# Loading one weight matrix in two transfers, split by partitions: 16 rows and 112 rows

## The chip, the cores and the metric

The kernel runs on one core of one Trainium2 chip. The metric is the device time of one execution in microseconds (us), as the median of several runs. The record sorts runs into a fast and a slower state. The engines are called PE (matmuls), DVE (VectorE), ACT (ScalarE), POOL (GpSimd) and SP (SyncE, which here only issues transfers). The page of the profile counts 16 DMA engines, and they carry out a large transfer side by side: in `before` the first 16 rows of the first one begin between 1.84 and 2.78 us, each of them before any row has ended (3.27 us). In this text a "row" of a transfer is what goes to one partition of the on-chip memory (SBUF).

## The reference, cut to what matters

One decode step of a transformer block for eight sequences: a modulation (adaLN) from a condition `c`, attention over a key and value cache of 8192 positions, and a small MLP.

```python
mod = (_silu(c) @ w_mod).reshape(8, 6, 1, -1)          # w_mod: 512 x 3072, bf16, 3 MB
sa, ca, ga, sb, cb, gb = (mod[:, i] for i in range(6))
h = layernorm(x) * (1 + ca) + sa
x = x + ga * attention(h, k_cache, v_cache, wq, wo)    # caches: 2 x 8 x 8 x 8192 x 128, bf16, 268 MB
h = layernorm(x) * (1 + cb) + sb
return x + gb * mlp(h, w1, b1, w2, b2)
```

Nearly all of the bytes are the two caches. The modulation weights `w_mod` are about 1% of the total, and the change touches nothing but how they are loaded.

## The kernel before

The kernel streams everything through four slots of one SBUF buffer, `RING`, of 32 KB per partition and slot. SP issues the transfers in this order: `w_mod` into slot 2, `wq` into slot 3, the first two key units into slots 0 and 1, two small biases, `wo`, and then unit after unit as slots come free.

```python
d_wm = dma("sync", s_wm, lambda e: e.dma_start(
    RING[:, 2, 0:KT * NMOD], w_mod.rearrange("(p k) n -> p (k n)", k=KT)))
d_wq = dma("sync", s_wq, lambda e: e.dma_start(
    RING[:, 3, :], A_wq.rearrange("(p k) n -> p (k n)", k=KT)))
# ...
wmod_v = RING[:, 2, 0:KT * NMOD].rearrange("p (k n) -> p k n", k=KT)
# ... the first matmuls that need w_mod; they wait for all of it:
t = row_groups(bank(0), csT, wmod_v, (0, 1), [k_csT, d_wm])
k_mr0 = op("vector", lambda e: e.tensor_copy(mod_r[0:64, 0, :], bank(0)[0:64, :]), [t])
t = row_groups(bank(1), csT, wmod_v, (2, 3, 4, 5), [])
released[2] = t                      # slot 2 is free for the third key unit
# ...
t0 = row_groups(bank(2), haT, wq_v, (0, 1, 2, 3), [k_haT, d_wq])
# ...
load(0); load(1)                     # 4 MB key units
# ... two biases, wo
load(2); load(3)                     # these wait for released[2], released[3]
```

In `w_mod` each partition gets one contiguous row of 24,576 bytes (KT x NMOD = 4 x 3072 numbers of 2 bytes); in `wq` and in each cache unit it gets one row of 32,768 bytes. The helper `dma` adds 16 to the wanted value of its semaphore with every transfer, so two transfers on `s_wm` are waited for together: a wait for 32 passes only when both have landed.

## Time and profile before

| | before |
|---|---|
| time, median of 3 runs | 669.88 us (669.33 to 670.03) |
| span of the profiled run | 667.6 us |
| PE busy | 513.8 us (77%) |
| DMA moved | 283.85 MB, 425 GB/s over the span |
| `w_mod` landed, from issue | 10.3 us |

The page's slices come first: the span in 40 equal parts, the busy share of the 16 DMA engines in tenths, and the rate.

```profile
DMA  9999999999999999999999999999999999999996
GB/s 376 431 412 437 426 427 435 432 430 430 434 434 430 430 432 436 428 432 432 436 428 430 434 434 430 430 434 434 428 432 434 434 426 434 432 434 428 434 415 264
```

All slices but the last are at 90% or more, and the packets of SP's queue alone fill 99.1% of the 16 engines' span (packets, MB, share):

```profile
q1 hardware_dynamic: 12116, 283.65, 99.1%
```

That points to the transfers as what sets the time. The page's chain of waits, followed back from the last instruction, is less plain, for by shares PE has more of it than the transfers:

```profile
PE 52%; DMA 37%; ACT 7%; DVE 2%; SPq 1%; issue 1%
```

Shares can't decide it, because SP's queue is full while PE works. The longest links of the chain are these; the columns are start in us, length in us, and what was waited for.

```profile
1.26 13.33 DMA ring<-in_A_wq_dram
14.59 46.84 DMA ring<-in_A_k_cache_dram
...
95.68 24.03 DMA ring<-in_A_k_cache_dram
...
561.59 24.42 DMA ring<-in_A_k_cache_dram
...
649.42 14.74 DMA ring<-in_B_w_dram
```

At the beginning and in every batch (one sequence) the longest link is a wait for key data, and the chain ends in a wait for the last weights of the MLP, `B_w`. SP issues far ahead: a key load lands 34 us after its issue (the page's list of transfers). So the engines always have work queued.

The timeline shows the start: start in us, length in us, engine, line, operation, what it writes and reads, and in brackets how long the engine had been idle and for whom.

```profile
0.81 0.39 SPq L286 DMA_DIRECT2D ring<-in_w_mod_dram  x1
...
1.26 0.42 SPq L288 DMA_DIRECT2D ring<-in_A_wq_dram  x1
...
11.33 3.21 PE L398 MATMUL PS<-ring,KTb 128*32 128x512 bf16 x24
...
21.27 3.36 PE L398 MATMUL PS<-ring,KTb 128*32 128x512 bf16 x32 [3.76 <-DMA ring<-in_A_wq_dram]
...
30.71 5.53 PE L479 MATMUL PS<-IDENT,ring 128*128 128x128 bf16 x64 [5.12 <-DMA ring<-in_A_k_cache_dram]
```

The modulation matmuls (the first line of PE, L398) start at 11.33 us, those with `wq` at 21.27, and the first key tiles at 30.71. The list of transfers has these two entries (KB, and us from issue to landing):

```profile
ring<-in_A_wq_dram SPq DMA_DIRECT2D x1, 4096.0 KB, 19.9
...
ring<-in_w_mod_dram SPq DMA_DIRECT2D x1, 3072.0 KB, 10.3
```

Last, the same stretch in windows of 4 us; the last two columns are the DMA engines' busy share and the rate.

```profile
core 0: us, PE busy (x) PEld busy (x) DVE busy (x) ACT busy (x) POOL busy (x), PEclk, DMA share, GB/s
2.00:6.00 4.00, 0.29 (x4) 0.21 (x4) 0.85 (x2) 2.94 (x3) 3.38 (x9) 1.00 0.77 313
6.00:10.00 4.00, 0.27 (x4) 0.18 (x4) 1.18 (x5) 0.20 (x1) 3.71 (x3) 1.00 1.03 442
10.00:14.00 4.00, 3.24 (x26) 1.60 (x28) 1.35 (x3) 0.00 (x0) 2.58 (x11) 1.00 1.04 451
14.00:18.00 4.00, 3.51 (x22) 2.93 (x18) 1.08 (x5) 0.60 (x1) 2.19 (x12) 0.93 0.99 426
18.00:22.00 4.00, 0.73 (x8) 0.34 (x12) 0.00 (x0) 0.00 (x0) 2.26 (x12) 0.50 0.94 403
```

After a slow start the rate is that of the whole run. Below the views lie the records of the single packets; one packet is one row. They are given here as averages over 16 consecutive packets, that is about one row of each of the 16 engines:

```
before, w_mod (24,576 bytes each), us: 1.61 0.93 0.97 0.91 0.91 0.91 0.91 0.91
before, wq    (32,768 bytes each), us: 1.21 1.21 1.21 1.21 1.21 1.21 1.21 1.21
```

24,576 bytes in 912 ns are 26.9 GB/s for one engine and 431 GB/s for 16. No packet of the whole trace is faster than 27.04 GB/s, so each engine runs at the highest rate that is seen here, and nothing suggests that one hinders another. Only the first rows, at the start of the stream, take longer: 1.42 to 2.17 us, but for two of 0.99.

### The profile page before, as it was taken

The numbers are of one execution on the slowest core, as the hardware profiler recorded it, in microseconds if no ns is written. First come the engines' busy times: TensorE is split into PE (matmuls) and PEld (weight loads), VectorE is DVE, ScalarE is ACT, GpSimd is POOL, SyncE is SP. The second block draws the span as 40 slices with busy tenths as digits, with TensorE's granted clock in tenths as the row PEclk, the third lists the DMA queues.
The fourth block names the chain that finished last, engine by engine and source line by source line (L and its number), as shares of the span: only waits on it lengthen the run. The fifth ranks groups of instructions, "written<-read, shape, count | busy, mean of one in ns | idle before, by whom it ended". The sixth has DMA issues, their size and how long they took to land.

```text
span 667.6 us, 15485 instructions
## 1 busy us (share of the span) xinstructions
PE 513.8 (77%) x7064; PEld 344.8 (52%) x7064; DVE 302.6 (45%) x571; ACT 258.7 (39%) x289; POOL 18.4 (3%) x76
## 2 busy tenths in 40 slices
PE   3493984898739985699848987499756998389885
PEld 2283731675328742577317853287425773177534
DVE  2262731566216651367314662166513673156722
ACT  2151640466105660266404662066502654046610
POOL 7300000000000000000000000000000000000000
PEclk9696997899969998699977999699987999779996
DMA  9999999999999999999999999999999999999996
GB/s 376 431 412 437 426 427 435 432 430 430 434 434 430 430 432 436 428 432 432 436 428 430 434 434 430 430 434 434 428 432 434 434 426 434 432 434 428 434 415 264
DMA packets 12176, 283.85 MB, mean 425 GB/s; under 512 B 1250, under 2 KB 1283, under 8 KB 3588
## 3 DMA queue, kind: packets, MB, share of 16 engines
q1 hardware_dynamic: 12116, 283.65, 99.1%
q8 instruction: 9, 0.15, 0.1%
q10 hardware_dynamic: 48, 0.02, 0.0%
q14 instruction: 3, 0.02, 0.0%
HBM read 283.66 MB, written 0.01 MB: 425 GB/s over the span
## 4 chain that ended last, share of the span: by engine, by line
PE 52%; DMA 37%; ACT 7%; DVE 2%; SPq 1%; issue 1%
PE PS L479 36%; DMA ring<-in_A_k_cache_dram 32%; PE PS L496 9%; ACT P_sb L562 5%; PE PS L616 2%; DMA ring<-in_B_w_dram 2%; DMA ring<-in_A_wq_dram 2%; PE PS L469 1%; SPq L659 1%; ACT KTb L484 1%; DVE O_sb L626 1%; PE PS L463 1%; PE PS L574 1%; DVE Pm L588 0%; PE PS L594 0%
## 5 line engine op out<-in xcount | busy, mean ns | idle before, releaser
L484 ACT ACTIVATE KTb<-PS 128x1024 bf16<-128x1024 bf16 x192 | 196.5, 1024 | 332.2 <-PE PS L479 332.2
L479 PE MATMUL PS<-IDENT,ring 128*128 128x128 bf16 x4096 | 267.4, 227 | 51.2 <-DMA ring<-in_A_k_cache_dram 51.2
L479 PEld LDWEIGHTS PS<-IDENT,ring 128*128 128x128 bf16 x4096 | 246.8, 102 | 99.6 <-DMA ring<-in_A_k_cache_dram 52.4
L486 DVE COPY KTb<-PS 128x1024 bf16<-128x1024 bf16 x320 | 210.1, 687 | 143.9 <-PE PS L479 141.8
L616 PE MATMUL PS<-ring,Pm 128*32 128x512 bf16 x992 | 70.4, 434 | 46.8 <-DMA ring<-in_A_v_cache_dram 45.9
L496 PE MATMUL PS<-KTb,Qb 128*32 128x512 bf16 x1024 | 78.8, 385 | 4.5 <-ACT KTb L484 4.5
L626 DVE CAST O_sb<-PS 128x512 bf16<-128x512 f32 x31 | 21.4, 692 | 126.7 <-PE PS L616 126.7
L616 PEld LDWEIGHTS PS<-ring,Pm 128*32 128x32 bf16 x992 | 26.8, 106 | 85.5 <-DMA ring<-in_A_v_cache_dram 54.4
L562 ACT ACTIVATE P_sb<-PS,negm 128x1024 bf16<-128x1024 f32 x32 | 35.2, 1112 | 20.2 <-DVE negm L557 20.2
L469 PE MATMUL PS<-ONES 128*128 128x512 f32 x80 | 42.1, 630 | 0.0
L574 PE MATMUL PS<-IDENT,P_sb 128*128 128x128 bf16 x256 | 19.9, 220 | 15.4 <-ACT P_sb L562 15.4
L588 DVE COPY Pm<-PS 64x512 bf16<-64x512 bf16 x48 | 20.2, 421 | 25.0 <-PE PS L574 24.5
L574 PEld LDWEIGHTS PS<-IDENT,P_sb 128*128 128x128 bf16 x256 | 14.4, 98 | 25.1 <-ACT P_sb L562 25.1
L463 PE MATMUL PS<-IDENT 128*128 128x512 bf16 x88 | 26.9, 380 | 0.0
L496 PEld LDWEIGHTS PS<-KTb,Qb 128*32 128x32 bf16 x1024 | 15.4, 94 | 21.1 <-ACT KTb L484 8.5
L503 DVE TENSOR_REDUCE m<-PS 128x1 f32<-128x512 f32 x32 | 22.0, 689 | 6.6 <-PE PS L496 6.6
L630 PEld LDWEIGHTS PS<-SEL,O_sb 128*128 128x128 bf16 x124 | 5.8, 97 | 30.5 <-DVE O_sb L626 30.5
L469 PEld LDWEIGHTS PS<-ONES 128*128 128x128 f32 x80 | 12.7, 190 | 10.6 <-issue 10.6
L630 PE MATMUL PS<-SEL,O_sb 128*128 128x8 bf16 x124 | 7.9, 169 | 12.4 <-DVE O_sb L626 12.0
L641 DVE TENSOR_TENSOR oTn<-PS,rinv 128x8 f32 x31 | 6.0, 194 | 14.9 <-PE PS L630 14.9
L463 PEld LDWEIGHTS PS<-IDENT 128*128 128x128 bf16 x88 | 7.7, 105 | 9.1 <-issue 7.2
L484 ACT ACT_TABLE_LOAD x8 | 10.3, 1283 | 3.2 <-issue 3.2
(132 smaller groups left out, 115.9 us busy)
## 6 DMA issues: line engine op xcount, KB each, us to landing
ring<-in_A_k_cache_dram SPq DMA_DIRECT2D x32, 4096.0 KB, 34.2
ring<-in_A_v_cache_dram SPq DMA_DIRECT2D x31, 4096.0 KB, 27.8
ring<-in_A_wq_dram SPq DMA_DIRECT2D x1, 4096.0 KB, 19.9
wo_sb<-in_A_wo_dram SPq DMA_DIRECT2D x1, 4096.0 KB, 47.6
ring<-in_w_mod_dram SPq DMA_DIRECT2D x1, 3072.0 KB, 10.3
ring<-in_A_v_cache_dram SPq DMA_DIRECT2D x1, 2048.0 KB, 22.6
ring<-in_B_w_dram SPq DMA_DIRECT2D x3, 512.0 KB, 19.4
ring<-in_B_w_dram SPq DMA_DIRECT2D x1, 1344.0 KB, 17.9
```

What stands on the lines that cost most here:

```text
L463: ts = [op("tensor", lambda e: e.matmul(bank(at).rearrange("p (a r) -> p a r", a=4), IDENT[:, :], rhs)) for _ in range(n)]
L469: ts = [op("tensor", lambda e: e.matmul(bank(at).rearrange("p (a r) -> p a r", a=4), ONES[:, :], rhs)) for _ in range(n)]
L479: t = op("tensor", lambda e, j=j, i=i: e.matmul(STG[j][:, i, :], src[:, 32 * k + 8 * j + i, :], IDENT[:, :], is_transpose=True), [loaded[n ...
L484: stg_free[j] = op("scalar", lambda e, j=j, dst=dst: e.activation(dst, STG[j], ACT.Copy), [t])
L486: stg_free[j] = op("vector", lambda e, j=j, dst=dst: e.tensor_copy(dst, STG[j]), [t])
L496: t = op("tensor", lambda e, hf=hf, q=q, rhs=rhs: e.matmul(PS[32 * q:32 * (q + 1), k, :], Qb[:, 2 * p + hf, :], rhs, start=(p == 0 and hf ...
L503: return op("vector", lambda e: e.tensor_reduce(m4[:, k:k + 1], bank(k), AX.X, ALU.max), [t])
L562: exps.append(op("scalar", lambda e, k=k: e.activation(P_sb[:, k, :, :, :], bank(k).rearrange("p (i x) -> p i x", i=8).unsqueeze(2).to_bro ...
L574: t = op("tensor", lambda e, k=k, i=i: e.matmul(STG[k][:, i, :], P_sb[:, k, i, :, :].rearrange("p h x -> p (h x)"), IDENT[:, :], is_transp ...
L588: done.append(op("vector", lambda e, dst=dst, frm=frm: e.tensor_copy(dst, frm), [t, k_pm]))
L616: t = op("tensor", lambda e, p=p, m=m, cg=cg, vt=vt, Obank=Obank: e.matmul(Obank[32 * cg:32 * (cg + 1), :], lhs[:, p, 32 * m:32 * m + 32], ...
L626: t = op("vector", lambda e, osb=osb, Obank=Obank: e.tensor_copy(osb, Obank), [t])
```

## The change

The modulation weights come in two transfers instead of one: first the first 16 partitions, one row for each DMA engine, then the other 112. Such a split might be meant to get the first bytes moving sooner. The bytes, their source and their destination are the same.

```diff
-        d_wm = dma("sync", s_wm, lambda e: e.dma_start(
-            RING[:, 2, 0:KT * NMOD], w_mod.rearrange("(p k) n -> p (k n)", k=KT)))
+        wmod_p = w_mod.rearrange("(p k) n -> p (k n)", k=KT)
+        for a, z in ((0, 16), (16, 128)):
+            d_wm = dma("sync", s_wm, lambda e, a=a, z=z: e.dma_start(
+                RING[a:z, 2, 0:KT * NMOD], wmod_p[a:z]))
```

## The prediction

The sum came to +5.3 us on 669.9. The 5.5 us of the slowest engine, the mean of 3 us, the spread of 4 us and the range are estimates. The picture behind them: engines which write certain partitions at the same moment slow each other.

> **What bounds the kernel now.** The transfers. The page's slices show the DMA engines at 90% or more in 39 of 40 slices, 425 GB/s over the span; PE is 77% busy and waits for key data: the longest links of the chain of waits are key loads (a first one of 46.8 us, then about 24 us in each batch). In the trace's packet records the 16 engines run without a gap from 1.84 us to about 662 us: a 24,576-byte row takes 912 ns (16 such: 431 GB/s), a 32,768-byte row 1,213 to 1,221 ns. SP issues far ahead (34 us from issue to landing of a key load), so a delay of an engine's stream is never made good: it comes out at the last weight load, which ends the chain (14.7 us, then 5 us of PE and output).
>
> **What the change does.** It moves the same 3 MB into the same rows in 128 packets. It adds one issue on SP (0.39 us in the timeline) and 16 semaphore packets of 9 ns. The modulation matmuls still wait for both transfers. Releasing slot 2 later does no harm: wq, two key units and wo, 16 MB or 39 us, are queued without it.
>
> What moves is which row each engine writes when. [...] In before each engine runs at its full rate[...]; no large partial transfer is in this trace. [...]
>
> **Cost[...].**
> - First transfer: [...] The first rows of before took 1.4 to 2.2 us, so some hides in the start: -0.5.
> - Second: if each engine takes seven consecutive rows[...]
> - Earlier first byte: 0.1 to 0.2 us.
>
> The slowest engine is about 5.5 us late; landings wait for it and nothing later has slack, so all of it lies on the critical path. Total 669.9 + 5.3 = 675.2 us, 0.8% slower.
>
> **Prediction: 675.2 us, range 670.2 to 681.5. Faster by over 2%: 0.005; within 2%: 0.895; slower by over 2%: 0.10.**
>
> **What would show it.**
> - Packets of the first transfer take 3 to 4 us; some of the second 1.8 us or more; all later ones 1.21 us.
> - In the timeline the modulation matmuls start at 15 to 17 us instead of 11.33, the query matmuls at about 26 instead of 21.3; the first key tiles, every later batch and the last weight load shift by the same 4 to 6 us.
> - The engines' finishing times spread over some 4 us instead of 0.94.
> - PE, DVE and ACT busy times are unchanged.
>
> **What would make it wrong.** [...] If late engines can catch up, the loss shrinks to their mean, about 3 us.

## The result and the profile after

| | before | after |
|---|---|---|
| time, median of 4 runs | 669.86 us | 675.67 us (675.12 to 675.97) |
| ratio | | 1.0087 (95% interval 1.007 to 1.0105) |
| span of the profiled run | 667.6 us | 673.3 us |
| PE, DVE, ACT busy | 513.8, 302.6, 258.7 us | 517.4, 302.5, 258.9 us |
| last packet of `wq` ended (trace time) | 20.4 us | 26.1 us |

Ratios here and below are the mean time of one kernel's fast runs over that of the other's fast runs of the same rounds, so they are not quite the ratio of the medians. Where this text gives a loss of an experiment in us, it is (ratio - 1) times 670.

The change makes the kernel 5.8 us slower, 0.9%, which is within 2%. The page's slices of after:

```profile
DMA  9999999999999999999999999999999999999996
GB/s 233 425 414 434 433 424 433 434 434 432 424 434 432 430 436 432 432 430 428 432 430 436 432 434 432 426 432 428 436 432 434 432 426 432 430 434 432 434 413 265
```

Only the first of 40 slices has changed much: 233 GB/s instead of 376 over about 17 us. The engines are still at 90% of busy time there. They were not idle; they took longer for the same bytes. The windows of the first 22 us show it in detail (columns as before):

```profile
2.00:6.00 4.00, 0.29 (x4) 0.21 (x4) 0.86 (x2) 2.95 (x3) 3.38 (x9) 1.00 0.81 141
6.00:10.00 4.00, 0.26 (x4) 0.18 (x4) 0.41 (x2) 0.00 (x0) 3.71 (x3) 1.00 1.05 291
10.00:14.00 4.00, 0.64 (x4) 0.55 (x4) 1.35 (x5) 0.20 (x1) 2.62 (x11) 1.00 1.05 276
14.00:18.00 4.00, 0.97 (x10) 0.43 (x12) 0.00 (x0) 0.00 (x0) 2.25 (x12) 1.00 0.87 303
18.00:22.00 4.00, 4.00 (x29) 2.08 (x21) 0.68 (x1) 0.60 (x1) 2.28 (x13) 1.00 1.11 477
```

From 2 to 14 us the rate is between 141 and 291 GB/s, where before reached 442 and 451 from 6 us on. From 18 us on the rate is no longer lower than before. The timeline:

```profile
0.81 0.85 SPq L288 DMA_DIRECT2D ring<-in_w_mod_dram  x2
...
1.71 0.42 SPq L290 DMA_DIRECT2D ring<-in_A_wq_dram  x1
...
17.03 3.60 PE L400 MATMUL PS<-ring,KTb 128*32 128x512 bf16 x24 [4.61 <-DMA ring<-in_w_mod_dram]
...
26.83 3.60 PE L400 MATMUL PS<-ring,KTb 128*32 128x512 bf16 x32 [3.23 <-DMA ring<-in_A_wq_dram]
...
36.45 4.77 PE L481 MATMUL PS<-IDENT,ring 128*128 128x128 bf16 x43 [5.03 <-DMA ring<-in_A_k_cache_dram]
```

The modulation matmuls start 5.7 us later, the `wq` matmuls 5.6 us later and the first key tiles 5.7 us later. The list of transfers shows the two parts and `wq` behind them, which takes 5.1 us longer from issue to landing and is issued 0.45 us later:

```profile
ring<-in_A_wq_dram SPq DMA_DIRECT2D x1, 4096.0 KB, 25.0
...
ring<-in_w_mod_dram SPq DMA_DIRECT2D x1, 2688.0 KB, 15.7
...
ring<-in_w_mod_dram SPq DMA_DIRECT2D x1, 384.0 KB, 5.6
```

And the chain of waits:

```profile
1.71 18.97 DMA ring<-in_A_wq_dram
20.68 46.23 DMA ring<-in_A_k_cache_dram
...
102.03 23.35 DMA ring<-in_A_k_cache_dram
...
568.07 23.64 DMA ring<-in_A_k_cache_dram
...
653.16 16.06 DMA ring<-in_B_w_dram
```

The long links are the same as before; the waits for key data that are shown end 5.5 to 5.7 us later. The last link, the wait for `B_w`, ends at 653.16 + 16.06 = 669.22 us instead of 649.42 + 14.74 = 664.16, 5.1 us later; the remaining 0.6 us are one more group of 16 matmuls that still had to be done after it. So the loss of the first 17 us stood at the end of the kernel almost unchanged. Nothing made it good, and nothing made it worse.

The packet records of after, averaged over 16 as above (the first number is the 16-row transfer, the next seven are the 112 rows):

```
after, w_mod (24,576 bytes each), us: 2.30 2.15 1.52 1.42 1.30 1.35 1.57 1.57
after, wq    (32,768 bytes each), us: 1.71 1.22 1.22 1.24 1.21 1.22 1.22 1.22
```

Every group of 16 rows of `w_mod` takes longer on average, and so does the first of `wq`, which is written while other engines are still busy with `w_mod` (the first row of `wq` begins at 14.61 us, the last of `w_mod` ends at 16.18). After that nearly all is as before. The sum agrees: the times of all packets of SP's queue, added up and divided by 16, rose from 661.8 to 667.5 us. Of these 5.7 us, 5.1 lie in the packets of `w_mod` and 0.5 in the first 128 rows of `wq`. The number of semaphore packets of 4 bytes in that queue rose from 1,226 to 1,242: the added transfer has 16 of them, as many as there are engines, and its 16 rows begin between 1.84 and 2.82 us, before any has ended (3.26 us). So 16 engines work on the small transfer as on the large one.

### The profile page after: what moved, and what is told of

Same layout as the page of the kernel before. It is cut to its first block, busy times and chain, and to the rows that moved or that the text cites. A ratio compares the mean times of both kernels' runs of the same rounds, so it can differ in the third digit from the quotient of the medians.

```text
span 673.3 us, 15486 instructions
## 1 busy us (share of the span) xinstructions
PE 517.4 (77%) x7064; PEld 347.1 (52%) x7064; DVE 302.5 (45%) x571; ACT 258.9 (38%) x289; POOL 18.6 (3%) x76
## 4 chain that ended last, share of the span: by engine, by line
PE 52%; DMA 37%; ACT 7%; DVE 2%; SPq 1%; issue 1%
PE PS L481 36%; DMA ring<-in_A_k_cache_dram 32%; PE PS L498 9%; ACT P_sb L564 5%; DMA ring<-in_A_wq_dram 3%; DMA ring<-in_B_w_dram 2%; PE PS L618 2%; PE PS L471 1%; ACT KTb L486 1%; SPq L661 1%; DVE O_sb L628 1%; PE PS L465 1%; PE PS L576 1%; DVE Pm L590 0%; PE PS L596 0%
## 5 line engine op out<-in xcount | busy, mean ns | idle before, releaser
L400 PE MATMUL PS<-ring,KTb 128*32 128x512 bf16 x56 | 7.2, 626 | 7.8 <-DMA ring<-in_w_mod_dram 4.6
```

## The experiments

Three theories were tested.

- **A, the writing side.** Engines that write certain partitions at the same moment ("meet") slow each other.
- **B, the reading side.** The split changes which rows of HBM are read side by side, and that costs time.
- **C, the second transfer.** One more issue, one more set of semaphore packets and a small transfer at the head of the stream cost the time.

All 12 runs differ from the changed kernel only in how `w_mod` (in one case `wq`) is loaded (only112 also clears the rows that it doesn't load), and each was timed in three rounds against the kernel before, with that kernel's runs on the same chip.

| run | partitions of each transfer | packet in the steady part, us | last packet of `wq`, us later than before | loss, us |
|---|---|---|---|---|
| cols2 | 128, half of the columns, twice | 0.46 (half rows) | -0.3 | 0.0 |
| eight_adj | 16 adjacent, 8 times | 3.26 | 17.9 | 18.4 |
| eight_adjsrc_spreaddst | every 8th, 8 times | 1.91 | 7.3 | 7.1 |
| eight_spreadsrc_adjdst | 16 adjacent, 8 times, other sources | 3.29 | 18.2 | 18.0 |
| halves | 64 adjacent, twice | 1.92 | 7.7 | 7.9 |
| even_odd | every 2nd, twice | 0.91 | 0.3 | 0.2 |
| quarters_adj | 32 adjacent, 4 times | 1.91 | 7.1 | 7.9 |
| quarters_spread | every 4th, 4 times | 0.91 | 0.3 | 0.4 |
| split96_32 | 96, then 32 | 1.64 to 1.90 | 6.8 | 7.2 |
| last16 | 112, then 16 | 1.2 to 1.7, then 2.9 | 6.5 | 7.0 |
| only112 | 112 (16 not loaded) | 1.4 to 1.7 | 3.0 | 3.1 |
| wq_16_112 | `wq` in 16 and 112 | 2.1 to 2.3 (32 KB rows) | 10.8 | 10.4 |

The last two columns are worth a look before the single runs. The first is read at about 20 to 40 us, the second at the end, and in every run they agree within 0.8 us, from 0 up to 18 us. That is the rule "what an engine loses early comes out at the end", shown for this kernel over the whole range. (A ratio's interval is about 1.1 us to either side, so losses that differ by less than that are not told apart.)

### Is it the second transfer, the reading or the writing?

**cols2.** The split is made along the columns, so each of the two transfers goes to all 128 partitions.

```diff
-        for a, z in ((0, 16), (16, 128)):
-            ... e.dma_start(RING[a:z, 2, 0:KT * NMOD], wmod_p[a:z])
+        for a, z in ((0, HALF), (HALF, 2 * HALF)):          # HALF = KT * NMOD // 2
+            ... e.dma_start(RING[:, 2, a:z], wmod_p[:, a:z])
```

> The weights come in two transfers of all 128 partitions, each with half of the columns (12 KB of every row). Correct result. Theory A[...]: no meeting, so 669.9 us as before, within 0.7. Theory B (the loss is on the reading side, in which rows of HBM are read side by side): the same rows side by side as before, also 669.9. Theory C (a second transfer costs it: issue, semaphores, start): 675.7 as in the changed kernel.

Measured: 669.87 us, ratio 1.0000 (0.9984 to 1.0017), the result correct. The second transfer costs nothing that can be seen: theory C falls, but for its small transfer at the head, which last16 tests below. The modulation matmuls start at 10.85 us.

**eight_adj** has eight transfers of 16 adjacent partitions, which takes the 16-row part of the change to its extreme.

```diff
-        for a, z in ((0, 16), (16, 128)):
-            ... e.dma_start(RING[a:z, 2, 0:KT * NMOD], wmod_p[a:z])
+        for i in range(8):
+            ... e.dma_start(RING[16 * i:16 * i + 16, 2, 0:KT * NMOD], wmod_p[16 * i:16 * i + 16])
```

> Eight transfers of 16 adjacent rows into 16 adjacent partitions. Correct result. Theory A: [...] 669.9 + 21.9 = 691.8, less about 0.5 hidden in the start; packets of 3 to 4 us. Theory B: adjacent rows read side by side in each transfer, some loss, no size from me. Theory C: seven extra transfers instead of one, 7 x 5.8 = 40 us slower, 710.

Measured: 687.98 us, ratio 1.0274 (1.0257 to 1.0291), correct. The rows take 3.26 us each (0.91 in before), and the loss is 18.4 us instead of the 21.9 expected; 16 x 24,576 bytes in 3.264 us are 120 GB/s. The size that was expected was the author's estimate, and it was too large. Why was not shown. By their semaphore packets the engines are 1.07 us out of step, so for a part of the time two transfers are written at once, and other runs have shorter rows where one transfer runs into the next (1.77 us in halves, 1.75 in quarters_adj, 1.66 in eight_adjsrc_spreaddst) than in the rest of the run (about 1.91).

**eight_adjsrc_spreaddst** and **eight_spreadsrc_adjdst** take reading and writing apart. The first reads from HBM what eight_adj reads, but writes to every eighth partition; the second writes where eight_adj writes, but reads every eighth row. Both give a wrong result, since rows land in partitions where they don't belong.

```diff
+            ... e.dma_start(RING[i:128:8, 2, 0:KT * NMOD], wmod_p[16 * i:16 * i + 16])    # adjsrc_spreaddst
+            ... e.dma_start(RING[16 * i:16 * i + 16, 2, 0:KT * NMOD], wmod_p[i:128:8])    # spreadsrc_adjdst
```

> As the eight transfers of adjacent rows, same reads from HBM, but each is written to every eighth partition. The result is wrong on purpose (rows land in other partitions). Theory A: [...] 669.9 + 7.3 = 677.2, packets of about 1.8 us. Theory B: the reads are those of the eight adjacent transfers, so the same time as that run. Theory C: 710.

> Eight transfers that each read every eighth row of HBM and write 16 adjacent partitions. The result is wrong on purpose. Theory A: the writes are those of the eight adjacent transfers, so their time: 691.8, packets of 3 to 4 us. Theory B: the reads are spread, so little or no loss against before or at least another time than the adjacent reads. Theory C: 710.

Measured: 676.98 us (ratio 1.0106, 1.0089 to 1.0122) and 688.30 us (ratio 1.0269, 1.0252 to 1.0286). With the reads kept and the writes spread the loss falls from 18.4 to 7.1 us; with the writes kept and the reads spread it stays at 18.0. Theory B falls for such transfers of 16 rows: where the rows are written matters, and no effect of where they are read is seen. (For transfers of 112 or 96 rows reading and writing were not taken apart.) Theory A had expected 677.2 for the first. Two windows of each of the three runs, eight_adj first, then the two others in the order above:

```profile
6.00:10.00 4.00, 0.00 (x0) 0.00 (x0) 0.00 (x0) 0.00 (x0) 3.71 (x3) 1.00 0.85 100
10.00:14.00 4.00, 0.91 (x8) 0.73 (x8) 1.76 (x6) 0.20 (x1) 2.72 (x11) 1.00 1.03 123
```

```profile
6.00:10.00 4.00, 0.55 (x4) 0.55 (x4) 3.02 (x5) 0.20 (x1) 3.71 (x3) 1.00 0.93 203
10.00:14.00 4.00, 0.10 (x1) 0.00 (x1) 0.00 (x0) 0.00 (x0) 2.58 (x11) 1.00 0.96 197
```

```profile
6.00:10.00 4.00, 0.00 (x0) 0.00 (x0) 0.00 (x0) 0.00 (x0) 3.71 (x3) 1.00 0.86 100
10.00:14.00 4.00, 0.91 (x8) 0.73 (x8) 1.76 (x6) 0.20 (x1) 2.71 (x11) 1.00 0.93 111
```

The last column is about 100 to 120 GB/s where each transfer writes 16 adjacent partitions and about 200 where it writes every eighth one. (The windows count a packet's bytes at one moment, so a window of 4 us with packets of 3.3 us is coarse; the rate in the steady part is 120 from the packets of eight_adj, and 206 from those of the spread writes, 16 x 24,576 bytes in 1.91 us.)

### Is it a matter of the small first transfer?

**last16** turns the order round: `((0, 112), (112, 128))`.

> The split the other way round: first 112 partitions, then the last 16. Correct result. Theory A: the same meetings in another order; the 112 rows start together, the 16 rows at the end cost up to 2.3 us more than one row each (3.26 against 0.91), with nothing of it hidden in the start: 674 to 677. Rival, the small transfer at the head of the stream is the cause (it ends before the large one is under way): at most 1 us slower.

Measured: 676.48 us, ratio 1.0104 (1.0087 to 1.012), correct. The small transfer need not come first; at the end the loss is 7.0 us instead of 5.8, a difference about as wide as the intervals. The rival, that the small transfer at the head is the cause, falls.

**only112** leaves the first 16 partitions out; they are cleared by VectorE, so that the matmuls read zeros, and the result is wrong.

```diff
-        for a, z in ((0, 16), (16, 128)):
-            ... e.dma_start(RING[a:z, 2, 0:KT * NMOD], wmod_p[a:z])
+        d_wm = ... e.dma_start(RING[16:128, 2, 0:KT * NMOD], wmod_p[16:128])
+        k_ms = op("vector", lambda e: e.memset(RING[0:16, 2, 0:KT * NMOD], 0.0))
# ... and the first matmuls wait for k_ms too
```

> The transfer of the other 112 partitions alone; the first 16 are cleared by VectorE instead of loaded, so the result is wrong on purpose and 0.4 MB (0.9 us) less is moved. If the 112 rows lose by themselves as their packets say (about 1.5 us a row instead of 0.91, seven rows, and some of the first wq row): 669.9 - 0.9 + 4.2 = 673.2. If only the 16-row transfer loses: 669.0.

Measured: 672.68 us, ratio 1.0047 (1.003 to 1.0064). It moves 0.4 MB less, which at 431 GB/s is 0.9 us, and yet it is 3.1 us slower than before. So the 112 rows lose 3.1 + 0.9 = 4.0 us by themselves, and in the changed kernel the 16 rows add the other 5.8 - 4.0 = 1.8 us. (This assumes that the start hides as much of the one as of the other, which was not measured; and the interval of the 3.1 us is 2.0 to 4.3, so the two shares are known to about 1 us.)

**wq_16_112** leaves `w_mod` whole and splits `wq` in the same way. It is the second transfer, so its head is no longer the start of the stream.

```diff
+        d_wm = ... e.dma_start(RING[:, 2, 0:KT * NMOD], wmod_p)
+        for a, z in ((0, 16), (16, 128)):
+            d_wq = ... e.dma_start(RING[a:z, 3, :], wq_p[a:z])
```

> The modulation weights in one transfer; instead the query weights (4 MB, rows of 32 KB), which follow in the running stream, in one of 16 partitions and one of 112. Correct result. Theory A: the loss of the changed kernel (5.8) times 4/3, and nothing of it hidden in the start: 7.7 to 9, so 677.6 to 679; the modulation matmuls start as before at 11.3 us. Rival, the loss belongs to the start of the stream (first bytes, small first transfer): at most 1 us slower. Rival, engines that are late in the running stream catch up: under 4 us slower.

Measured: 680.29 us, ratio 1.0156 (1.014 to 1.0173), correct; 10.4 us of loss, more than the 7.7 to 9 expected. Two lines of its timeline and four of its windows:

```profile
13.31 3.60 PE L399 MATMUL PS<-ring,KTb 128*32 128x512 bf16 x24 [2.33 <-DMA ring<-in_w_mod_dram]
...
32.16 3.60 PE L399 MATMUL PS<-ring,KTb 128*32 128x512 bf16 x32 [12.28 <-DMA ring<-in_A_wq_dram]
```

```profile
14.00:18.00 4.00, 4.00 (x27) 1.92 (x22) 0.68 (x1) 0.60 (x1) 2.25 (x12) 1.00 0.74 172
18.00:22.00 4.00, 1.89 (x12) 1.75 (x12) 1.08 (x5) 0.00 (x0) 2.28 (x12) 0.83 1.01 248
22.00:26.00 4.00, 0.00 (x0) 0.00 (x0) 0.00 (x0) 0.00 (x0) 2.27 (x13) 0.50 1.11 262
26.00:30.00 4.00, 0.00 (x0) 0.00 (x0) 0.00 (x0) 0.00 (x0) 0.65 (x3) 0.50 0.98 246
```

The low rate sits exactly where `wq` is loaded, 172 to 262 GB/s from 14 to 30 us. So it isn't an effect of the start of the stream. On the contrary, the start may hide some of it: 5.8 us on a 3 MB load would be 7.7 on a 4 MB load, and 10.4 were measured. One detail was expected wrongly: the modulation matmuls started at 13.31 us, not at 11.3. The author's estimate, which was not tested, is that engines that finish `w_mod` early begin with the 16 rows of `wq` (in before the first row of `wq` begins 0.96 us before the last of `w_mod` ends), and that those slow the engines that still write `w_mod`: its last rows took up to 1.77 us in the packet records, and the last one ended 0.9 us later than before. The last semaphore update then came 1.65 us after that row, where it had been 0.35 in before; why was not tested.

### Which splits cost, and which don't?

**halves** splits at partition 64, `((0, 64), (64, 128))`.

> Two transfers of 64 adjacent partitions, four rows per engine. Correct result. Theory A, shares of adjacent rows (engine e has rows 4e to 4e+3): [...] as in the eight transfers to every eighth partition: rows of about 1.9 us, 7.4 us slower, 677. Theory A, rows dealt out in turn (e, e+16, ...): [...] rows of about 3.26 us, 18.4 us slower, 688. If only an uneven transfer of 112 rows loses: 669.9.

Measured: 677.96 us, ratio 1.0118 (1.0101 to 1.0135), correct; rows of 1.92 us. That is twice the 0.91 us of before: half of the rate.

**even_odd** uses transfers of 64 partitions too, but of every second one.

```diff
+        for i in range(2):
+            ... e.dma_start(RING[i:128:2, 2, 0:KT * NMOD], wmod_p[i:128:2])
```

> Two transfers of 64 partitions each, one the even partitions and one the odd. Correct result. [...] no loss, 669.9. [...] with four rows in a share (engine e starts at partition 8e) [...] rows of about 1.9 us, 7.4 us slower, 677.

Measured: 669.98 us, ratio 1.0003 (0.9987 to 1.002), correct; rows of 0.91 us from the second on. (In the expectation, 669.9 was for the case that it costs nothing to write every second partition; 677 was for theory A with four consecutive rows for each engine.) This is the run in which a guess of the prediction fell. If engine e had the e-th group of four rows, then the engines, as long as they kept step, would have written every eighth partition at one moment, as in eight_adjsrc_spreaddst, where the rows took 1.91 us. Here they took 0.91. So, if theory A holds, the rows of a transfer are not simply dealt out in consecutive groups. Nor do rows of 1.9 us follow just because only half of the partitions are written.

**quarters_adj** and **quarters_spread** repeat the pair with 32 partitions, adjacent ones (`32 * i:32 * i + 32`) and every fourth one (`i:128:4`).

> Four transfers of 32 adjacent partitions, two rows per engine[...]. Correct result. [...] rows of about 1.9 us as in the halves, 8 us slower, 678. If rows were dealt out in turn (e, e+16): [...] rows of 3.26 us, 688.

> Four transfers of every fourth partition, 32 rows each, two rows per engine[...]. Correct result. [...] as even and odd were: 669.9, rows of 0.91 us from the second on. If engine e simply has rows 2e and 2e+1 of the transfer: [...] 1.9 us, 677 to 678.

Measured: 677.39 us (ratio 1.0118, 1.0101 to 1.0134) and 669.89 us (ratio 1.0006, 0.999 to 1.0023), both correct. Two windows of quarters_spread, then two of halves:

```profile
6.00:10.00 4.00, 0.55 (x4) 0.55 (x4) 3.01 (x6) 0.20 (x1) 3.71 (x3) 1.00 0.93 393
10.00:14.00 4.00, 3.20 (x25) 1.03 (x24) 0.68 (x1) 0.00 (x0) 2.57 (x11) 1.00 1.03 442
```

```profile
6.00:10.00 4.00, 0.26 (x4) 0.18 (x4) 0.62 (x2) 0.00 (x0) 3.71 (x3) 1.00 1.00 209
10.00:14.00 4.00, 0.64 (x4) 0.55 (x4) 1.20 (x5) 0.20 (x1) 2.58 (x11) 1.00 0.95 197
```

At the same moments, with transfers that are only half as large, the spread quarters run at 393 to 442 GB/s and the adjacent halves at about 200.

**split96_32** has 96 partitions and then 32: `((0, 96), (96, 128))`.

> First 96 partitions (six rows per engine), then 32 (two rows per engine[...]). Correct result. The 32 rows cost 2 x (1.9 - 0.91) = 2 us. [...] the 96 are free: 672. If any share [...] loses as the 112 rows do (about 1.5 us a row instead of 0.91): 6 x 0.55 = 3.3 us more, 675.

Measured: 676.59 us, ratio 1.0107 (1.009 to 1.0123), correct: 7.2 us, more than either expectation (2 and 5). The packets of the 96 rows, averaged over 16 as before, take 1.55, 1.82, 1.68, 1.88, 1.64 and 1.88 us, those of the 32 rows 1.79 and 1.90. (The expectation of 672 had the 96 rows free, that of 675 had them lose as the 112 do.) So a row of a transfer to 96 adjacent partitions can lose nearly as much as one of a transfer to 64 (1.92 us in halves).

What stays open is how the 96 or 112 rows are dealt out to the 16 engines, and why they are slow. The packets can't show it, because they name neither the engine nor the partition. For these 112 rows, which are the larger part of the change's loss, the place of the writes as the cause is therefore argued and not shown; what is shown is that the rows lose by themselves (only112), and that splits of `w_mod` along the columns (cols2) or into every second or fourth partition lose nothing that can be seen.

No version beat the kernel before; the best ones, cols2, even_odd and quarters_spread, are equal to it.

## Why the prediction was right, point by point

The time was predicted as 675.2 us, and 675.67 was measured. Not all of the steps deserve that.

- **The transfers bound the kernel, and what an engine loses early is never made good: right.** In all 12 runs and in the changed kernel the loss at the last packet of `wq` is the loss at the end, within 0.8 us. With 18 us of delay it still holds.
- **The cause is which rows the engines write at the same moment: right for the 16 rows, not shown for the 112.** With transfers of 16 rows, spreading the writes alone takes away most of the loss (18.4 to 7.1 us), spreading the reads alone takes away nothing that can be seen (18.0), and a second transfer to all 128 partitions costs nothing that can be seen (cols2, 0.0 us). For the 112 rows see the last paragraphs on split96_32.
- **16 engines for each part: right.** The added transfer brought 16 semaphore packets (1,226 to 1,242).
- **Packets of 3 to 4 us in the first transfer: the size was off.** The first 16 packets took 1.4 to 2.96 us, 2.3 on average, and the last engine was done at 5.37 us. In a steady stream of such transfers (eight_adj) the rows take 3.26 us; here, with engines that start up to 1 us apart, even less. By only112 the first transfer costs 1.8 us, known to about 1 us; the estimate of it was within that.
- **The loss of the second transfer: the way in which it is shared out was wrong, and the size was right by luck.** The prediction had it fall unevenly, on some engines not at all. There is no such lucky engine. All rows of the 112 take 1.1 to 1.8 us once the first transfer is through, and the averages are 1.30 to 1.57. By only112 the term is 4.0 us, and all engines lose about as much. In the prediction the slowest engine is about 5.5 us late, and the mean of the whole loss over the engines is about 3 us (it says so under "What would make it wrong"); measured over the packets, that mean is 5.7. Seven consecutive rows for each engine was an assumption; if theory A holds, even_odd and quarters_spread speak against consecutive rows for their shapes.
- **Engines' finishing times spread over some 4 us: wrong.** By their semaphore packets, the engines finished `w_mod` within 1.57 us of each other (before: 0.97) and `wq` within 1.09 (before: 0.97). So the loss is shared out evenly, as the point above says.
- **Earlier first byte, 0.1 to 0.2 us: not there.** The first packet begins at 1.838 us instead of 1.842.
- **Later matmuls: right.** 17.03 us for the modulation (15 to 17 had been said), 26.83 for `wq` (about 26), and 5.7 us of shift for the first key tiles.
- **PE, DVE and ACT busy times unchanged: right but for PE, where it doesn't matter.** PE's rose by 3.6 us to 517.4; in cols2 it is 517.3 without any loss, and in eight_adj 514.2 with 18.4 us of loss.
- **Releasing slot 2 later does no harm: right, as far as it can be seen.** The rate is back to that of before from 18 us on.

So the close hit, 0.5 us, was in part luck. The prediction took the lateness of its slowest engine as the loss, and all engines turned out to be about that late, for a reason that its picture of the rows does not contain. Had the picture been right and the engines evened out, it would have been 3 us. The range, 670.2 to 681.5, was the honest part: it covered other ways of dealing out the rows which the trace of before could not exclude.

## What to carry to other kernels

When a profile shows the DMA engines busy all the time, as here (9 tenths in 39 of 40 slices), ask of every change to a transfer which partitions the engines write side by side; in this kernel the time lost there returned at the end (5.7 us at the last packet of `wq`, 5.8 us in the end), although the transfer is 1% of the bytes and 650 us away from the end. To cut a load like this one into parts, cut it along the free axis (cols2: 0.0 us lost), or take every second or fourth partition (0.2 and 0.4 us, within the intervals): four transfers of 32 spread partitions were free as far as can be seen, four of 32 adjacent ones cost 7.9 us. "Busy" is no measure of a transfer's rate: in the damaged stretch of halves the busy share was 1.00 and 0.95 at 209 and 197 GB/s (6 to 14 us), in before 1.03 and 1.04 at 442 and 451.
